# First unit of a fused attention, maxout and rational kernel: the order recomputed, some scaling and weight splitting given to GpSimd

## The chip, the cores and the metric

The kernel runs on one core of one Trainium2 chip. The metric is the device time of one execution in microseconds. The engines are named as the profile names them: PE is TensorE, DVE is VectorE, ACT is ScalarE, POOL is GpSimd, and SP is the engine whose queue issues most loads.

## What is computed

A banded attention (4 batches, 8 heads, 576 positions, 64 per head), whose output `x` goes through a maxout layer and then through a layer with a rational activation. All arithmetic is float32; inputs that the reference keeps as float64 arrive as 64-bit words.

```python
scores = scale * np.matmul(q, k.transpose(0, 1, 3, 2))
mask_plain = (rel >= 0) & (rel < window)                                      # heads 0..3
mask_dil = (rel >= 0) & (rel < window * dilation) & (rel % dilation == 0)     # heads 4..7
attn = np.exp(scores - max); attn = attn / (attn.sum(-1) + 1e-09); attn_out = attn @ v
x = attn_out.transpose(0, 2, 1, 3).reshape(B * S, H * D)                      # 2304 x 512
x = np.maximum(np.maximum(x @ w1, x @ w2), x @ w3) @ w_out                    # 768 wide
h = x @ w_in; P = a0 + a1*h + a2*h*h + a3*h*h*h; Q = 1 + |b0|*|h| + |b1|*h*h  # 2048 wide
out = (P / (Q + 1e-06)) @ w_out2
```

## The kernel before

**Units and parts.** The 2304 tokens of the maxout layer go in five units of 384 or 512. The attention goes in twelve parts of 192 positions, and each part in two groups: `p` (plain band, tiles of 128 queries, 6 of 96 columns) and `d` (dilated band, tiles of 96 queries, 8 of up to 80 columns). Unit 0 needs parts 0 and 1; parts 2 and 3, needed by unit 1, are done beside unit 0's matmuls. Units 1 to 4 follow a fixed pattern that the change leaves alone.

**Steps of a part and group**, with the lines of the kernel before: `S` scores on PE (mask L325, products L341), `MX` maximum on DVE (L369), `D` subtraction on DVE (L385), `E` exponentials on ACT (L393, L397), `SM` row sum on DVE (L404), `SB` scaling by the reciprocal of the sum (L408 to L411 on DVE, or L415 on ACT, one instruction for each tile), `X` transposes on PE (L424), `XC` copy out of PSUM (L433 on DVE or L435 on ACT), `V` products with the values on PE (L447, L455), `VH` and `VL` high and low part of the result (L472 on ACT, L476 on DVE). Part 0's scaled tile is `sb`, part 1 uses spare room in the tiles called `keys`.

**Weights.** Each of the 18 first weights and 6 output weights of the maxout layer arrives as 64-bit words (`L`, SP queue, L534). `up` (ACT, L547) and `bits` (two DVE instructions, L555 and L557) make float32 of it, `hi` (ACT, L571) its high part, `lo` (DVE, L579) the low part. Three matmuls on high and low parts (L597, L598, L599) make one product. `P:n` is such a product for weight n of unit 0, `M:n` the running maximum (ACT L617, DVE L619), `HH` and `HL` the split of the hidden values (L625, L629), `Y` and `YS` the output layer.

**What sets the order.** Unit 0 is written out by hand, word by word, in the table `START`: the words are issued in that order, and each engine runs its own instructions in that order. `W:n` puts 4n small matmuls on a constant tile (`warm`, L207) ahead of the next use of a PSUM bank. Loads of the first unit go through the SP queue and land in the order of issue. POOL has two memsets of zero columns in this stretch (L350: a part at the start of a batch has fewer key columns) and otherwise issues transfers later on.

Of the kernel before, what the change touches and what calls it, by code (L numbers as in the profile page):

```python
# [33 lines left out]


START = """
mk mkB T kp0 qp0 qd0 W:8 S0:p kd0 MX0:p kd1 E0:p W:4 S0:d,mm SM0:p MX0:d qd1 D0:d E0:d SB0:p S1:d
X0:p,1 L SM0:d MX1:d X0:p,0,pv up kp1 qp1 S1:p,mm SB0:d XC0:p,1 bits E1:d L up MX1:p D1:p
XC0:p,0 v0 X0:d,1,sc X0:d,0,pv XC0:d,0 XC0:d,1 W:2 V0:p,mm SB1:d V0:d,sc X1:d,1 bits qd2 v1 E1:p
X1:d,0,mm SM1:p hi lo L L qp2 SB1:p S2:d,pv XC1:d,1 X1:p,0 XC1:d,0 VH0:p VH0:d hi XC1:p,0 L  # L40
X1:p,1,mm VL0:p V1:d,mm L MX2:d up XC1:p,1 VL0:d V1:p,mm VH1:d bits VH1:p VL1:d S2:p VL1:p lo up hi
P:0 up MX2:p L P:1 E2:d lo bits P:2 hi M:0 k1 up bits L SB2:d M:1 lo bits P:3 L hi E2:p up M:2 lo L
bits L hi lo M:3 up HH:0 P:4 X2:d,1,mm bits hi qp3 up hi lo L X2:d,0,pv L SB2:p,act bits S3:p P:5 up
L M:4 lo XC2:d,1 L MX3:p P:6 X2:p,1 qd3 XC2:d,0 S3:d,pv L bits M:5 hi X2:p,0,mm up lo bits P:7 HL:0
up hi M:6 HH:1 lo bits MX3:d up hi XC2:p,0 lo hi L up bits lo M:7 E3:p P:8 P:9 hi bits lo M:8 up
P:12 L L hi bits E3:d lo hi SM3:d M:9 up lo HL:1 HH:2 up XC2:p,1 bits M:12 hi v2 bits L up hi
SB3:d,act P:10 lo M:10 up P:13 L bits P:11 M:13 L SM3:p P:14 V2:p,sc hi HL:2 V2:d,sc SB3:p,act M:11
lo X3:p,0 up lo bits L M:14 hi bits up X3:d,0,pv bits HH:4 XC3:p,0 L X3:d,1,mm hi X3:p,1,pv lo v3
HH:3 lo P:16 HL:4 hi XC3:d,1 lo up P:15 HL:3 up P:17 bits XC3:d,0 VH2:d M:15 bits up XC3:p,1 hi
VH2:p M:16 bits lo V3:p hi M:17 V3:d,tp lo VH3:p hi VH3:d lo HH:5 HL:5 Y:2 VL2:d VL3:d Y:0 YS:0 YS:2  # L50
Y:3 VL3:p YS:3 Y:1 VL2:p YS:1
"""

UNITS = {3: """
# [49 lines left out]
def kernel(  # L104
# [16 lines left out]
    nc = tc.nc  # L121
# [167 lines left out]
    def attn_pieces(c):  # L289
# [12 lines left out]
        def SC(g, pool="sc"):  # L302
            plain = g == "p"
            qT = at_raw.pop((c, g))
            U, Q, W = (2 * BP, 2 * QP, WP) if plain else (8, 2 * M, nmk)
            G = U // 2
            pem = on_pe(g)
            scs = []
            for j in range(2):
                t = bank(pool, "sc")  # L310
                ww = WP if plain else WD
                scs.append(t[:, 0:G * ww].rearrange("p (u w) -> p u w", w=ww)[:Q, :, :W])

# [13 lines left out]
            for n in range(U):
                i, blk = divmod(n, BP)
                if plain:
                    k0 = key0(ci, blk)  # L330
                    lq, rk = qT[:, n, :], kTp[:, k0 // 32:(k0 + WP) // 32, i, :]
                else:
                    lq, rk = qT[:, n, :], kTd[:, m0 // 16:(m0 + nmk) // 16, n, :]
                o = scs[n // G][:, n % G, :]
                o = o.rearrange("q (n t) -> q n t", t=32 if plain else 16)
                for h in (slice(0, QP), slice(QP, Q)) if plain else (slice(0, Q),):
                    if plain and c < EARLY:
                        l, r = lq[h], rk[h]
                    else:
                        l, r = lq[:, h], rk  # L340
                    nc.tensor.matmul(o[h], lhsT=l, rhs=r,  # L341
                                     start=not pem, stop=not pem or n % G == G - 1)
            if c == 1:
                ww = WP if plain else WD
                sb = keys0["x1l" if plain else "x1h"][:Q, 2 * S:2 * S + U * ww]
                sb = sb.rearrange("p (u w) -> p u w", w=ww)
            else:
                sb = at.tile([Q, U, WP if plain else WD], F32, tag="s" + g, bufs=SBB, name="sb")
            if W < WD and not plain:
                nc.gpsimd.memset(sb[:, :, W:WD], 0.0)  # L350
# [50 lines left out]
        def SM(g):  # L401
            sv, Q, W, U, sm = grp[g][:5]
            if mode[g] != "A":
                nc.vector.tensor_reduce(out=sm[:, :, 0], in_=sv, axis=AX.X, op=ALU.add)  # L404

        def SB(g, engine="dve"):
            sv, Q, W, U, sm = grp[g][:5]
            nc.vector.tensor_scalar_add(sm, sm, 1.0e-9)  # L408
            nc.vector.reciprocal(sm, sm)
            if engine == "dve":  # L410
                nc.vector.tensor_tensor(out=sv, in0=sv, in1=sm.to_broadcast([Q, U, W]),  # L411
                                        op=ALU.mult)
# [157 lines left out]
        cv[i][3] = slot  # L570
        nc.scalar.activation(out=slot[:, 0:512], in_=cv[i][2], func=AF.Copy)  # L571

    def cv_lo(i):
        kind, f, j = conv_seq[i]
        _, _, t, slot = cv.pop(i)
        if kind == "w2":
            nc.gpsimd.dma_start(out=w2d[f], in_=t)
        else:
            nc.vector.tensor_sub(slot[:, 512:1024], t, slot[:, 0:512].bitcast(F32))  # L579

    cv_at = {"load": 0, "up": 0, "bits": 0, "hi": 0, "lo": 0}
    cv_steps = (("hi", cv_hi, "bits"), ("lo", cv_lo, "bits"), ("up", cv_up, "load"),
# [112 lines left out]
    with ExitStack():  # L695
# [385 lines left out]
```

## Time and profile before

| | us |
|---|---|
| median of 3 runs | 776.62 (776.45 to 776.84) |
| the profiled execution | 776.12 |
| its span, first to last instruction | 774.3 |
| PE busy in the span | 766.6 (99%) |
| DVE, ACT, POOL busy | 585.3, 452.7, 59.3 |
| granted TensorE clock, all slices | 0.9 or more of full speed |

PE is listed as busy nearly throughout, but the ends of matmuls are modelled in this profile, so a wait is best seen in the distance between the starts of two groups. The chain of waits leads over PE for 97% of the span; the remaining 3% lie in the first 25 us, before the first product with a weight.

### The profile page before, as it was taken

Reading aid. Unit: us, or ns where it says so; the run is one execution under the profiler, and the core shown is the slowest. Engines: PE = TensorE matmul, PEld = TensorE weight load, DVE = VectorE, ACT = ScalarE, POOL = GpSimd, SP = SyncE. Lnnn points to the kernel's source line nnn. Section 1 sums busy time; section 2 is a strip of 40 time slices with the busy share of each in tenths; the row PEclk is TensorE's granted clock in tenths of the full one; section 3 lists DMA queues with packets and bytes.
Section 4 is the critical chain, followed back from the end, with each engine's and each line's share of the span. In section 5 each row is a group of like instructions: output and inputs, shape, how many; then the busy total and the mean of one; then the engine's idle time right before and its main releaser. Section 6 shows DMA issues by size and latency. Waiting matters only on the chain.

```text
span 774.3 us, 12063 instructions
## 1 busy us (share of the span) xinstructions
PE 766.6 (99%) x4656; PEld 660.3 (85%) x4656; DVE 585.3 (76%) x996; ACT 452.7 (58%) x842; POOL 59.3 (8%) x114
## 2 busy tenths in 40 slices
PE   8999999999999999999999999999999999999998
PEld 7999999988888888888888888888888888888996
DVE  6999477567635663455499998889888998888983
ACT  5997243433332333343687878677776768676872
POOL 0000222213121101000000001000000001000010
PEclk9999999999999999999999999999999999999999
DMA  9981577657655557532400011000110001000010
GB/s 344 401 347 50 181 226 239 198 157 234 193 176 173 170 177 237 186 109 92 139 0 1 1 55 55 1 1 3 66 42 1 1 28 55 1 0 1 1 55 27
DMA packets 28634, 85.67 MB, mean 111 GB/s; under 512 B 3680, under 2 KB 5728, under 8 KB 28576
## 3 DMA queue, kind: packets, MB, share of 16 engines
q1 hardware_dynamic: 19344, 52.08, 21.4%
q0 software_dynamic: 8800, 32.51, 11.5%
q8 instruction: 36, 0.59, 0.3%
q10 hardware_dynamic: 432, 0.31, 0.1%
q14 instruction: 22, 0.18, 0.1%
HBM read 67.06 MB, written 17.83 MB: 110 GB/s over the span
## 4 chain that ended last, share of the span: by engine, by line
PE 97%; ACT 1%; DVE 1%; DMA 0%; issue 0%; SPq 0%; ACTq 0%
PE mm L597 13%; PE mm L598 13%; PE mm L599 13%; PE h L597 8%; PE h L599 8%; PE h L598 8%; PE acc L909 8%; PE acc L911 8%; PE acc L910 8%; PE sc L341 3%; PE tpp L424 2%; PE pv L455 1%; PE pv L447 1%; DMA qTp<-in_qf_dram 0%; ACT keys L397 0%; DVE mx L369 0%
## 5 line engine op out<-in xcount | busy, mean ns | idle before, releaser
L597 PE MATMUL mm<-x1h,w1s 128*128 128x512 f32 (+1 forms) x360 | 134.5, 374 | 0.0
L599 PE MATMUL mm<-x1h,w1s 128*128 128x512 f32 (+1 forms) x360 | 132.4, 368 | 0.0
L598 PE MATMUL mm<-x1l,w1s 128*128 128x512 f32 (+1 forms) x360 | 132.4, 368 | 0.0
L599 PE MATMUL h<-x2h,w2s 128*128 128x512 f32 (+1 forms) x280 | 103.0, 368 | 0.0
L598 PE MATMUL h<-x2l,w2s 128*128 128x512 f32 (+1 forms) x280 | 103.0, 368 | 0.0
L597 PE MATMUL h<-x2h,w2s 128*128 128x512 f32 (+1 forms) x280 | 103.0, 368 | 0.0
L909 PE MATMUL acc<-w2s,gh 128*128 128x512 f32 x252 | 98.1, 389 | 0.0
L910 PE MATMUL acc<-w2s,gh 128*128 128x512 f32 x252 | 98.1, 389 | 0.0
L911 PE MATMUL acc<-w2s,gl 128*128 128x512 f32 x252 | 96.2, 389 | 0.0
L857 ACT ACTIVATE q<-h 128x512 f32<-128x512 f32 x72 | 43.1, 598 | 85.5 <-PE h L599 84.1
L597 PEld LDWEIGHTS mm<-x1h,w1s 128*128 128x128 f32 x360 | 67.6, 188 | 9.1
L599 PEld LDWEIGHTS mm<-x1h,w1s 128*128 128x128 f32 x360 | 67.6, 188 | 8.6
L864 DVE SCALAR_TENSOR_TENSOR q<-q,cs,ab 128x512 f32<-128x512 f32 x72 | 54.0, 749 | 27.5 <-ACT ab L858 26.6
L598 PEld LDWEIGHTS mm<-x1l,w1s 128*128 128x128 f32 x360 | 67.6, 188 | 8.1
L619 DVE TENSOR_TENSOR m<-mm,m 128x512 f32<-128x512 f32 (+1 forms) x60 | 38.0, 633 | 35.2 <-PE mm L599 30.5
L599 PEld LDWEIGHTS h<-x2h,w2s 128*128 128x128 f32 x280 | 52.8, 189 | 8.8
L597 PEld LDWEIGHTS h<-x2h,w2s 128*128 128x128 f32 x280 | 52.8, 189 | 8.8
L598 PEld LDWEIGHTS h<-x2l,w2s 128*128 128x128 f32 x280 | 52.7, 188 | 8.8
L859 ACT ACTIVATE p<-h,cs 128x512 f32<-128x512 f32 x72 | 56.5, 785 | 0.4 <-DVE gl L894 0.4
L911 PEld LDWEIGHTS acc<-w2s,gl 128*128 128x128 f32 x252 | 47.3, 188 | 9.9
L910 PEld LDWEIGHTS acc<-w2s,gh 128*128 128x128 f32 x252 | 47.3, 188 | 9.7
L909 PEld LDWEIGHTS acc<-w2s,gh 128*128 128x128 f32 x252 | 47.3, 188 | 9.7
(120 smaller groups left out, 1492.3 us busy)
## 6 DMA issues: line engine op xcount, KB each, us to landing
w1r<-in_w_dram SPq DMA_DIRECT2D x18, 512.0 KB, 9.2
raw<-in_w_in_dram SPq DMA_DIRECT2D x16, 512.0 KB, 4.3
w2d<-cvt POOLq DMA_DIRECT2D x32, 256.0 KB, 4.7
raw<-in_w_out_dram SPq DMA_DIRECT2D x16, 512.0 KB, 4.2
w2s<-w2d SPq DMA_DIRECT2D x28, 256.0 KB, 2.9
vd<-in_vd_dram POOLq DMA_DIRECT2D x8, 512.0 KB, 5.6
x2l<-x2d SPq DMA_DIRECT2D x4, 1024.0 KB, 6.0
out_dram<-ob POOLq DMA_DIRECT2D x16, 256.0 KB, 2.7
```

The costliest lines, as they stand in the source:

```text
L341: nc.tensor.matmul(o[h], lhsT=l, rhs=r, start=not pem, stop=not pem or n % G == G - 1)
L424: nc.tensor.transpose(tp[:, i, :], sv[:, G * j + i, :], ident[:Q, :Q])
L597: nc.tensor.matmul(o, lhsT=lh, rhs=rh, start=(i == 0), stop=False)
L598: nc.tensor.matmul(o, lhsT=lh, rhs=rl, start=False, stop=False)
L599: pe_at[0] = nc.tensor.matmul(o, lhsT=ll, rhs=rh, start=False, stop=(i == n - 1))
L619: nc.vector.tensor_tensor(out=m1[u, f], in0=o, in1=m1[u, f], op=ALU.max)
L857: nc.scalar.activation(out=s["q"], in_=s["h"], func=AF.Square)
L859: nc.scalar.activation(out=s["p"], in_=s["h"], func=AF.Identity, scale=cs[:, 3:4], bias=cs[:, 2:3])
L864: nc.vector.scalar_tensor_tensor(out=s["q"], in0=s["q"], scalar=cs[:, 5:6], in1=s["ab"], op0=ALU.mult, op1=ALU.add)
L909: nc.tensor.matmul(o, lhsT=gh, rhs=w[:, 0:512], start=(c == 0), stop=False)
L910: nc.tensor.matmul(o, lhsT=gh, rhs=w[:, 512:1024], start=False, stop=False)
L911: nc.tensor.matmul(o, lhsT=gl, rhs=w[:, 0:512], start=False, stop=(c == F2 - 1))
```

## The change

The table `START` is replaced by another order of the same words. Four things in the code go with it: `SB` can run its large multiplication on POOL, and does so for both groups of parts 0, 2 and 3 (six multiplications; the addition and the reciprocal stay on DVE); `lo` can run on POOL, and does so for weights 0, 1, 3, 4, 5, 6 and 7; part 3's zero columns are written by DVE behind its row sum, no longer by POOL at its scores; and one copy `XC0:p,0` moves from ACT to DVE. Before, `SB` of part 2 `p` and of part 3 `p` and `d` was on ACT, the others on DVE. The words `W` make 52 small matmuls, 56 before. From the end of unit 0 on, nothing is changed.

```diff
 START = """
-mk mkB T kp0 qp0 qd0 W:8 S0:p kd0 MX0:p kd1 E0:p W:4 S0:d,mm SM0:p MX0:d qd1 D0:d E0:d SB0:p S1:d
+mk mkB T qp0 kd0 kp0 qd0 kd1 qd1 W:8 S0:p qp1 kp1 L MX0:p S0:d,mm W:3 S1:d,pv MX0:d D0:d W:1 S1:p,mm
...
-            if W < WD and not plain:
+            if W < WD and not plain and c != 3:
                 nc.gpsimd.memset(sb[:, :, W:WD], 0.0)
...
             if mode[g] != "A":
                 nc.vector.tensor_reduce(out=sm[:, :, 0], in_=sv, axis=AX.X, op=ALU.add)
+                if c == 3 and g == "d":
+                    nc.vector.memset(grp[g][8][:, :, W:WD], 0.0)
...
-            if engine == "dve":
-                nc.vector.tensor_tensor(out=sv, in0=sv, in1=sm.to_broadcast([Q, U, W]),
-                                        op=ALU.mult)
+            if engine != "act":
+                engine = nc.vector if engine == "dve" else nc.gpsimd
+                engine.tensor_tensor(out=sv, in0=sv, in1=sm.to_broadcast([Q, U, W]), op=ALU.mult)
                 return
...
-    def cv_lo(i):
+    def cv_lo(i, engine=nc.vector):
...
-            nc.vector.tensor_sub(slot[:, 512:1024], t, slot[:, 0:512].bitcast(F32))
+            engine.tensor_sub(slot[:, 512:1024], t, slot[:, 0:512].bitcast(F32))
...
-                    cv_step(op)
+                    cv_step(op, *[nc.gpsimd] * (arg == "pool"))
```

POOL, from its first memset of zero columns to its first transfers; `w1s` is a split weight, `cvt` its float32 form, `sm` the reciprocals. Before:

```order
L350 MEMSET sb 96x8x32 x2
L653 DMA x2d<-xs 128x384 x2
L283 DMA vp_1296<-in_vp_dram 128x768
L284 DMA vd_1297<-in_vd_dram 128x1024
L653 DMA x2d<-xs 128x384 x2
```

And in the change:

```order
L350 MEMSET sb 96x8x32
L414 ISA
L414 TENSOR_TENSOR sb<-sb,sm 128x576
L414 TENSOR_TENSOR sb<-sb,sm 96x8x48
L581 TENSOR_TENSOR w1s_0_454<-cvt,w1s_0_454 128x512
L581 TENSOR_TENSOR w1s_1_519<-cvt,w1s_1_519 128x512
L414 TENSOR_TENSOR sb<-sb,sm 96x640
L581 TENSOR_TENSOR w1s_0_617<-cvt,w1s_0_617 128x512
...
L414 TENSOR_TENSOR sb<-sb,sm 128x576
L655 DMA x2d<-xs 128x384 x2
```

Thirteen two-input instructions now stand ahead of POOL's first transfer, with one instruction listed as ISA in front of them (the built program names it a reload of POOL's library).

DVE, from the maxima of part 0 (`sc` is a score tile) to the scaling of part 1. Before:

```order
L369 TENSOR_REDUCE mx<-sc 128x3 x2
L372 TENSOR_SCALAR mx<-mx 128x6
L404 TENSOR_REDUCE sm<-sb 128x6
L369 TENSOR_REDUCE mx<-sc 96x4 x2
L385 TENSOR_TENSOR sb<-sc,mx 96x4x48 x2
L408 TENSOR_SCALAR sm<-sm 128x6
L409 RECIPROCAL sm<-sm 128x6
L411 TENSOR_TENSOR sb<-sb,sm 128x576
L404 TENSOR_REDUCE sm<-sb 96x8
L369 TENSOR_REDUCE mx<-sc 96x4 x2
```

And in the change:

```order
L369 TENSOR_REDUCE mx<-sc 128x3 x2
L372 TENSOR_SCALAR mx<-mx 128x6
L369 TENSOR_REDUCE mx<-sc 96x4 x2
L385 TENSOR_TENSOR sb<-sc,mx 96x4x48 x2
L404 TENSOR_REDUCE sm<-sb 128x6
L410 TENSOR_SCALAR sm<-sm 128x6
L411 RECIPROCAL sm<-sm 128x6
L369 TENSOR_REDUCE mx<-sc 96x4 x2
L372 TENSOR_SCALAR mx<-mx 96x8
L404 TENSOR_REDUCE sm<-sb 96x8
```

The two multiplications of part 0 are gone from DVE, and the maxima and differences of part 0's dilated group stand ahead of the plain group's row sum.

SP, its first loads (`qTp`, `qTd` are queries, `keys` the keys of the first batch). Before:

```order
L246 DMA keys_146<-in_kp_dram 128x384
L262 DMA qTp_149<-in_qf_dram 128x384
L262 DMA qTd_151<-in_qd_dram 128x768
L250 DMA keys_147<-in_kd_dram 128x384
L250 DMA keys_147<-in_kd_dram 128x768
L262 DMA qTd_250<-in_qd_dram 128x768
L534 DMA w1r_0_276<-in_w_dram 128x512
L246 DMA keys_146<-in_kp_dram 128x768
```

And in the change:

```order
L262 DMA qTp_146<-in_qf_dram 128x384
L250 DMA keys_149<-in_kd_dram 128x384
L246 DMA keys_148<-in_kp_dram 128x384
L262 DMA qTd_152<-in_qd_dram 128x768
L250 DMA keys_149<-in_kd_dram 128x768
L262 DMA qTd_155<-in_qd_dram 128x768
L262 DMA qTp_208<-in_qf_dram 128x384
L246 DMA keys_148<-in_kp_dram 128x768
```

The first six loads are the same six in another order; behind them part 1's plain queries and keys now come before the first weight.

## Rows read from the trace of the kernel before

**Rows 1.** The page: span; busy time by engine; the chain by engine.
```profile
span 774.3 us, 12063 instructions
...
PE 766.6 (99%) x4656; PEld 660.3 (85%) x4656; DVE 585.3 (76%) x996; ACT 452.7 (58%) x842; POOL 59.3 (8%) x114
...
PE 97%; ACT 1%; DVE 1%; DMA 0%; issue 0%; SPq 0%; ACTq 0%
```

**Rows 2.** Timeline of PE: start, us, engine, line, tiles, count, idle before and releaser.
```profile
9.28 1.55 PE L341 MATMUL sc<-keys,qTd 128*96 128x80 f32 x16 [0.33 <-DMA qTd<-in_qd_dram]
11.48 0.86 PE L424 MATMUL tpp<-mk,sb 128*96 128x128 f32 x6 [0.65 <-DVE sb L411]
...
14.35 0.83 PE L424 MATMUL tpp<-mk,sb 96*80 96x96 f32 x8 [0.63 <-ACT keys L397]
...
16.46 0.92 PE L447 MATMUL pv<-pt,vp 96*64 96x64 f32 x24 [0.83 <-ACT pt L435]
...
19.24 1.51 PE L341 MATMUL sc<-keys,qTd 128*96 128x80 f32 x16
21.04 0.83 PE L424 MATMUL tpp<-mk,keys 128*96 128x128 f32 x6 [0.28 <-ACT w1s L571]
...
25.12 0.45 PE L597 MATMUL mm<-x1h,w1s 128*128 128x384 f32 x1
```

**Rows 3.** The chain that ended last, in order of time: start, us, what.
```profile
4.98 1.22 PE sc L341 x24
...
6.99 1.51 ACT sb L397 x6
...
42.71 1.32 PE sc L341 x16
```

**Rows 4.** Busy time by stretch: length, PE, PEld, DVE, ACT, POOL, clock, DMA, GB/s.
```profile
9.28:25.12 15.84, 13.44 (x234) 11.92 (x234) 15.39 (x40) 12.24 (x37) 0.00 (x0) 1.00 1.03 404
25.12:50.00 24.88, 24.88 (x178) 24.42 (x177) 24.23 (x54) 22.79 (x70) 0.31 (x1) 1.00 1.03 404
50.00:75.00 25.00, 25.00 (x242) 24.29 (x240) 24.59 (x51) 22.59 (x59) 0.00 (x0) 1.00 0.35 123
```

**Rows 5.** Groups of DVE by form, 9.28 to 75 us: busy, mean ns, idle.
```profile
L557 DVE SCALAR_TENSOR_TENSOR cvt<-w1r,cvt 128x512 int32<-128x512 int32 x18 | 12.5, 693 | 0.6
L579 DVE TENSOR_TENSOR w1s<-cvt,w1s 128x512 fp32r<-128x512 f32 x18 | 12.2, 680 | 0.0
L555 DVE TENSOR_SCALAR cvt<-cvt 128x512 int32<-128x512 int32 x24 | 10.0, 417 | 0.0
L619 DVE TENSOR_TENSOR m<-mm,m 128x384 f32<-128x384 f32 x12 | 6.6, 547 | 0.0
L557 DVE SCALAR_TENSOR_TENSOR cvt<-wo1r,cvt 128x512 int32<-128x512 int32 x6 | 4.2, 692 | 0.2
L579 DVE TENSOR_TENSOR wo1s<-cvt,wo1s 128x512 fp32r<-128x512 f32 x6 | 3.9, 683 | 0.0
...
L411 DVE TENSOR_TENSOR sb<-sb,sm 96x640 f32<-96x640 f32 x1 | 0.8, 821 | 0.1
...
L411 DVE TENSOR_TENSOR sb<-sb,sm 128x576 f32<-128x576 f32 x1 | 0.8, 759 | 0.0
...
L411 DVE TENSOR_TENSOR sb<-sb,sm 96x384 f32<-96x384 f32 x1 | 0.6, 553 | 0.0
```

**Rows 6.** Groups of ACT by form in the same stretch.
```profile
L415 ACT ACTIVATE sb<-sb,sm 128x96 f32<-128x96 f32 x12 | 3.4, 362 | 0.9 <-DVE sm L409 0.9
```

**Rows 7.** Groups of POOL by form, from the start to 75 us.
```profile
L350 POOL MEMSET sb<- 96x256 f32 x2 | 0.6, 308 | 35.8 <-PE tpp L424 35.5 <-POOLq L1064 0.3
...
L1064 POOL MEMSET const-float32-0.0<- 128x1 f32 x1 | 0.1, 104 | 0.2 <-issue 0.2
```

**Rows 8.** Timeline of POOL at 237 us: a transfer that it issues.
```profile
237.35 0.55 POOL L653 DMA_DIRECT2D x2d<-xs  x1 [4.48 <-ACT xs L652]
```

**Rows 9.** Timeline of DVE at the same moment.
```profile
237.63 0.49 DVE L555 TENSOR_SCALAR cvt<-cvt 128x512 int32<-128x512 int32 x1 [0.33 <-ACT cvt L547]
```

More of the change, by code (lines that the diff above doesn't have):

```diff
@@ L36 @@
 START = """
-mk mkB T kp0 qp0 qd0 W:8 S0:p kd0 MX0:p kd1 E0:p W:4 S0:d,mm SM0:p MX0:d qd1 D0:d E0:d SB0:p S1:d
[L38 to L48, printed above, removed]
@@ L49 @@
-HH:3 lo P:16 HL:4 hi XC3:d,1 lo up P:15 HL:3 up P:17 bits XC3:d,0 VH2:d M:15 bits up XC3:p,1 hi
-VH2:p M:16 bits lo V3:p hi M:17 V3:d,tp lo VH3:p hi VH3:d lo HH:5 HL:5 Y:2 VL2:d VL3:d Y:0 YS:0 YS:2
-Y:3 VL3:p YS:3 Y:1 VL2:p YS:1
+mk mkB T qp0 kd0 kp0 qd0 kd1 qd1 W:8 S0:p qp1 kp1 L MX0:p S0:d,mm W:3 S1:d,pv MX0:d D0:d W:1 S1:p,mm
+E0:p E0:d SM0:p SB0:p,pool X0:p,1 qd2 MX1:d SM0:d SB0:d,pool MX1:p X0:p,0,mm D1:p XC0:p,0,dve E1:d
+W:1 X0:d,0,sc v0 E1:p XC0:p,1 L v1 up qp2 X0:d,1,mm S2:d,pv XC0:d,0 SB1:d SM1:p L XC0:d,1 X1:d,0
@@ new lines @@
+V0:p,mm SB1:p V0:d,sc XC1:d,0 L VH0:p X1:p,0,mm X1:p,1 up XC1:p,0 X1:d,1,sc XC1:p,1 XC1:d,1 VH0:d
+bits VL0:p qp3 hi V1:p,mm bits VL0:d lo:pool VH1:p V1:d,tp S2:p VL1:p VH1:d up VL1:d L L hi k1 up
+MX2:d MX2:p E2:d qd3 bits bits lo:pool hi P:0 SB2:d,pool L lo L P:1 up L bits M:0 S3:p,pv up bits hi
+MX3:p lo:pool hi lo:pool L P:2 L E2:p L P:3 up hi M:1 M:2 up S3:d,mm M:3 bits X2:d,1,sc bits X2:d,0
+hi HH:0 lo:pool up P:4 L MX3:d lo:pool SB2:p,pool E3:d up bits hi HL:0 hi lo:pool XC2:d,0 SM3:d M:4
@@ new lines @@
+bits L P:5 P:6 X2:p,1 hi lo up M:5 X2:p,0,sc lo bits up up L L bits hi E3:p hi M:6 P:7 P:9 lo
+XC2:p,0 SB3:d,pool L v2 bits SM3:p XC2:p,1 lo M:7 P:10 hi up up HH:1 lo bits hi L M:9 SB3:p,pool
+P:11 up bits M:10 lo bits hi P:8 M:11 P:12 L up L hi HH:3 XC2:d,1 lo M:8 lo V2:d,sc bits up V2:p,sc
+bits M:12 hi lo X3:p,1,pv VH2:d up up X3:d,0,pv X3:d,1,mm hi X3:p,0 L HL:1 bits lo bits hi XC3:d,1
+up P:15 HH:2 L hi lo bits lo L P:13 up XC3:p,0 bits M:15 XC3:d,0 up HL:2 M:13 VH2:p hi bits hi L hi
+lo v3 P:14 M:14 P:16 lo M:16 up P:17 bits lo M:17 HH:4 XC3:p,1 V3:p,tp hi HH:5 V3:d VH3:p HL:3 VH3:d
@@ L52 @@
+HL:4 HL:5 lo Y:2 VL3:p Y:1 YS:2 Y:3 YS:1 VL2:d VL2:p VL3:d Y:0 YS:3 YS:0
 """
@@ L719, with cv_step @@
         steps = {n: (fn, after) for n, fn, after in cv_steps}
-        def cv_step(name):
+        def cv_step(name, *engine):
             fn, after = steps[name]
@@ L724, in cv_step @@
             assert name != "lo" or cv_at["lo"] < cv_at["hi"]
-            fn(cv_at[name])
+            fn(cv_at[name], *engine)
             cv_at[name] += 1
```

## The prediction, made before the changed kernel ran

> **What bounds the kernel now.** I read the page first: PE works for 99% of the span and the chain of waits runs over PE for 97% of it [rows 1]. So time can only be won where PE waits, and the profiled execution took 776.12 us, of which 774.3 are span and 1.8 lie around it. Next I read PE's timeline for waits. All that are listed lie ahead of 25.12 us, where PE meets the first product with a weight [rows 2]; after that no matmul waits for another engine. What the reader is to see in rows 2 is the distance between starts, since the ends of matmuls are modelled. Last I read the busy time by stretch: from 25 to 75 us DVE works 24.23 of 24.88 and 24.59 of 25.00 us, and ACT 22.8 and 22.6 [rows 4]. PE doesn't wait there, but the engine that feeds it has no room. Moving anything in this stretch is therefore a matter of DVE's instructions, one by one.
>
> **The start of the gain: PE's waits ahead of the first product.** The two orders can be compared from 9.28 us on, where PE takes up the second dilated scores as their queries land [rows 2]. The same six loads stand ahead of that point in both orders, so the transfers set it alike. Between 9.28 and 25.12 us PE does the same work in both: scores of part 1 and 2, transposes and products of parts 0 and 1, and eight small matmuls. Before, it waited four times in between. The sixteen score matmuls take 1.32 us when nothing follows late [rows 3]. Between 9.28 and 11.48 that leaves 2.20 - 1.32 = 0.88 us for DVE's scaling of part 0. Then 0.63 us are listed for part 1's exponentials and 0.83 us for the copy of the transposed tile. Between 19.24 and 21.04 there are 1.80 - 1.32 = 0.48 us for the next transposes [rows 2]. The sum is 2.82 us. In the new order the first transposes come only behind all scores of part 1, the copies behind those of part 2, and so on: each wait has other PE work in its place. **2.8 us is the most that can be won,** since the load sets 9.28 us and PE is full afterwards.
>
> Ahead of 9.28 us something gets worse and costs nothing. Part 0's plain scores now need the third load of the queue, not the second: 128 x 384 words of 4 bytes are 0.197 MB, at 404 GB/s 0.49 us [rows 4], so they begin at 4.98 + 0.49 = 5.47 us [rows 3]. PE still reaches the second dilated scores before their queries, as the 0.33 us idle there show [rows 2]: the new order has 12 small matmuls there where the old has 16.
>
> **What is given back on PE's path.** No row of before shows POOL reading two tiles, so its price is bounded by what POOL does show: a memset of 96x256 takes 0.308 us and one of a single column 0.104 [rows 7], so a column written costs (0.308 - 0.104) / 256 = 0.80 ns. An instruction with two inputs and one output makes one such pass if the three overlap and three if they don't: for 512 columns 0.51 to 1.33 us, for 576 columns 0.56 to 1.49, for 384 columns 0.41 to 1.03, for 640 columns 0.62 to 1.64. DVE takes 0.680, 0.759, 0.553 and 0.821 for these [rows 5]. Two of POOL's scalings and two of its low parts lie on PE's way to the first product:
> - Part 0 plain: its exponentials end at 6.99 + 1.51 = 8.50 us [rows 3], so now at 9.0. Behind the row sum (as long as a scaling, 0.76) and two short DVE instructions, themselves behind the dilated group's differences, POOL starts at an estimated 10.4 and ends by 11.0 to 11.9. PE comes to these transposes at 9.28 + 1.32 + 1.22 = 11.8 us and, with the small matmuls and the mask in between, about 12.3, behind part 1's plain scores [rows 3]. Hidden, with 0.4 us left at the worst end.
> - Part 0 dilated: its scaling starts at an estimated 12.8 us, behind a maximum of part 1 on DVE, and PE wants it at about 13.2, after the transposes of 0.86 [rows 2]. It ends at 13.2 to 13.8, so the wait is 0 to 0.6; I take 0.15.
> - The low parts of weights 0 and 1: 0.51 to 1.33 for 0.68, from -0.2 to +0.65 ahead of the first product; I take 0.15.
>
> Together 0.3 us (bounds -0.2 to 1.3, since chained steps may miss each other).
>
> **Beside PE's path: DVE and ACT.** DVE loses 7 low parts x 0.680, and scalings of 0.759, 0.553 and 0.821: 6.89 us [rows 5]. It gains part 3's zero columns (0.31 by POOL's row, rows 7) and a copy out of PSUM (0.55, as the maximum from PSUM, rows 5): 6.0 us less in all. ACT loses three scalings, of six or eight instructions of 0.36 us each, some 5 to 7 us [rows 6]. The price is nothing as long as POOL is the cover, and POOL was idle there [rows 4]. So PE's demand, 2.5 us earlier than before, finds its weights ready unless POOL slows DVE down. The zero columns on DVE stand behind a row sum; had they stayed on POOL, they would hold up the scalings behind them.
>
> **Do POOL and DVE disturb each other?** One row of before shows it: while POOL issued a transfer at 237.35, a conversion on DVE took 0.49 us, where the mean is 0.417 [rows 5, 8, 9]: 0.07 us more. Nine of POOL's thirteen instructions fall behind 25 us, and DVE's conversions are 12.5 + 12.2 + 10.0 + 4.2 + 3.9 = 42.8 us of its 64.2 in the stretches of rows 4, or 67% [rows 5]. At 0.07 us for each that meets one, that is 9 x 0.07 x 0.67 = 0.4 us. I take this, because it is the only row in which the two meet. The far bound is the first rival.
>
> The sum: -2.8 + 0.3 + 0.4 = -2.1 us. The median of before is 776.62, 0.5 us above the profiled execution, and the change is put against the median: **774.5 us.**
>
> **The rivals.**
> *POOL and DVE exclude each other* (slower). If a POOL instruction with two inputs shuts out DVE's conversions and low parts for its whole length, DVE loses 67% of POOL's time behind 25 us. At the upper bounds that time is 5 x 1.33 + 1.64 + 1.49 + 1.03 + 1.49 = 12.3 us, so 8.2 us lost against 6.0 us of relief: DVE, which had no room, is 2.2 us later than before and PE with it, 776.6 + 2.2 = 778.8 us. At the lower bounds (4.7 us) it loses 3.2, and the gain stands. It decides at 6.0 / 0.67 = 9.0 us, 1.0 us an instruction: above it the kernel is slower. For it speaks that POOL's memset rate makes more than one pass likely, and that the low parts follow the conversions closely. Against it: the one meeting in the rows cost 0.07 us, not the rest of POOL's 0.55.
> The Trainium skill has this very rule (SBUF — State Buffer, Who interferes with whom): a DVE instruction with two SBUF inputs contends with a GpSimd instruction that reads SBUF, and whichever starts first holds the shared port to its end. No run here shows that pair yet. The skill also puts a two-input GpSimd instruction at about 2.6 cycles an element (GPSIMD Engine Reference, Elementwise), an estimate of 1.1 us and more for 512 columns; by both the rival's time would be about 778.
>
> *POOL begins late* (slower). The ISA instruction ahead of POOL's first multiplication isn't in the trace of before. POOL is free from the end of its first memset at 1.1 us, and is needed at 10.4 us, so up to 9.3 us of it is hidden, and 0.4 to 1.3 us more by the room above. Each us beyond goes onto PE's path one for one; above some 12.5 us the kernel is slower, and at 15 us it would be about 779.
> The Trainium skill gives about 6 us for the first call into freshly loaded code on this engine (GPSIMD Engine Reference, Instruction dispatch); by that the load is hidden.
>
> *The waits come back under other names* (no change). The dependencies between 12 and 28 us are close in the new order (the copy that moves to DVE, part 1's scalings, the first low parts). If four of them miss by 0.4 us each, 1.6 of the 2.8 us are gone: 775.5 to 776.5.
>
> **How the numbers follow.** A difference of 0.2% is 1.55 us and about what a measurement of this kernel can tell from none. The forecast, a gain of 1.6 to 2.9 us, has a chance of 0.43. Exclusion has 0.37, of which 0.27 is slower by over 1.55 us and 0.10 lies within, at shorter instructions. The late start has 0.06, slower. Waits that come back have 0.14, within. So faster 0.43, same 0.24, slower 0.33. The forecast's own range is 773.7 to 775.1. The range of 8 in 10 must take in most of exclusion: from 773.4, just past the most that can be won, to 779.6, just past exclusion at its upper bounds; a late start and a longer exclusion lie outside.
>
> **What would show it.** Right: PE's timeline takes up the second dilated scores at about 9.3 us again, has no wait over 0.6 us behind that, and meets the first product at about 22.5 us; POOL's thirteen instructions take 0.5 to 1.5 us each; DVE's conversions keep 0.417 and 0.693 us, and DVE has some 5 us idle up to 75 us. Wrong by exclusion: DVE rows for L557, L559 and L581 (their lines in the change) start late or last over 1 us while POOL works, and PE waits for DVE between 27 and 60 us. Wrong by a late start: POOL's first multiplication starts behind 11 us and PE waits for it. Wrong by returning waits: the first product at 24 us or later.

## The result, and the profile after

The changed kernel takes **780.61 us** in the median of 6 runs (779.6 to 781.41), against 776.54 us before, in the median of the 6 runs beside it; the ratio is 1.0054, with a 95% interval from 1.0041 to 1.0067. It is slower by about 4.1 us, where 774.5 us were forecast, and the range (773.4 to 779.6) does not hold it. The profiled execution took 780.62 us, 778.9 of them span; the span is 4.6 us longer than that of [rows 1].

Helpers' lines moved by two: the conversions are now L557 and L559, the low parts L581, the scalings L414, the maxima of the products L621. First the engines from 25 to 75 us, by stretch, and their sum and mean over the four (after, then before; columns as in [rows 4]).

```profile
25.00:35.00 10.00, 9.30 (x69) 8.25 (x68) 9.79 (x17) 8.75 (x37) 5.29 (x4) 1.00 1.03 400
35.00:45.00 10.00, 7.64 (x48) 7.45 (x48) 9.69 (x20) 6.18 (x18) 5.18 (x4) 0.83 1.03 409
45.00:57.00 12.00, 11.95 (x71) 11.58 (x71) 11.73 (x24) 9.40 (x22) 1.70 (x2) 1.00 0.78 311
57.00:75.00 18.00, 17.96 (x154) 17.43 (x153) 17.73 (x34) 14.50 (x30) 0.28 (x1) 1.00 0.30 96
sum 50.00, PE 46.85 PEld 44.71 DVE 48.94 ACT 38.84 POOL 12.45; mean PE 11.71 PEld 11.18 DVE 12.23 ACT 9.71 POOL 3.11
```
```profile
25.00:35.00 10.00, 10.00 (x63) 9.88 (x59) 9.69 (x21) 9.67 (x39) 0.00 (x0) 1.00 1.03 400
35.00:45.00 10.00, 10.00 (x92) 9.54 (x91) 9.76 (x23) 8.54 (x20) 0.31 (x1) 1.00 1.03 408
45.00:57.00 12.00, 12.00 (x71) 11.95 (x70) 11.76 (x26) 11.59 (x32) 0.00 (x0) 1.00 0.88 346
57.00:75.00 18.00, 18.00 (x202) 17.34 (x200) 17.73 (x36) 15.70 (x40) 0.00 (x0) 1.00 0.19 53
sum 50.00, PE 50.00 PEld 48.72 DVE 48.94 ACT 45.50 POOL 0.31; mean PE 12.50 PEld 12.18 DVE 12.23 ACT 11.37 POOL 0.08
```

DVE's column is the one to read. It is busy for 48.94 of 50 us in both, but in that time it works on 92 instructions, where before it was 103 (counted over the 50 us as one stretch; in the rows above, one that crosses a bound stands twice). POOL works 12 us longer, and DVE is no less busy for it. PE, which had no gap here, loses 3.15 us.

The timelines of DVE and of POOL (after, 29 to 36 us) show where it goes: start, duration, engine, line.

```profile
29.19 0.42 DVE L557 TENSOR_SCALAR cvt<-cvt 128x512 int32<-128x512 int32 x1
29.64 1.63 DVE L559 SCALAR_TENSOR_TENSOR cvt<-w1r,cvt 128x512 int32<-128x512 int32 x1
31.20 1.50 DVE L557 TENSOR_SCALAR cvt<-cvt 128x512 int32<-128x512 int32 x1
32.73 1.66 DVE L559 SCALAR_TENSOR_TENSOR cvt<-w1r,cvt 128x512 int32<-128x512 int32 x1
34.32 0.81 DVE L369 TENSOR_REDUCE mx<-sc 128x3 f32<-128x288 f32 x2
35.16 1.27 DVE L372 TENSOR_SCALAR mx<-mx 128x6 f32<-128x6 f32 x1
```
```profile
28.88 1.84 POOL L414 TENSOR_TENSOR sb<-sb,sm 96x640 f32<-96x640 f32 x1 [3.56 <-DMA qTd<-in_qd_dram]
30.69 3.16 POOL L581 TENSOR_TENSOR w1s<-cvt,w1s 128x512 fp32r<-128x512 f32 x2
35.13 1.27 POOL L581 TENSOR_TENSOR w1s<-cvt,w1s 128x512 fp32r<-128x512 f32 x1 [1.29 <-ACT w1s L573]
```

The conversions took 0.417 and 0.693 us in [rows 5]; the last three here take 1.50 and 1.63 to 1.66, and each ends 0.4 to 0.6 us behind the end of a POOL instruction (30.72, about 32.3, 33.85), as if it began only then. The engines take turns: POOL's pair at 30.69 needs 1.58 us each, where one takes 1.28 when DVE doesn't meet it. Even L372, six numbers a partition, lasts 1.27 us, to just behind POOL's end at 36.40.

What reads PSUM is not held (DVE, then POOL, at 44 us): the maximum L621 lies wholly inside POOL's subtraction and takes 0.48 us, no more than the 0.547 of [rows 5]; the conversion behind it is held to 0.75 us and ends 0.29 us behind POOL.

```profile
44.12 0.48 DVE L621 TENSOR_TENSOR m<-mm,m 128x384 f32<-128x384 f32 x1
44.53 0.75 DVE L557 TENSOR_SCALAR cvt<-cvt 128x512 int32<-128x512 int32 x1
```
```profile
43.70 1.29 POOL L581 TENSOR_TENSOR w1s<-cvt,w1s 128x512 fp32r<-128x512 f32 x1 [1.26 <-ACT w1s L573]
```

PE's longest wait is for DVE (PE's waits by releaser: total, times, longest).

```profile
PE sc L325 <- DVE m L621: 2.9, 2, 2.4
PE sc L341 <- DMA keys<-in_kp_dram: 1.2, 1, 1.2
PE sc L207 <- DVE warm L699: 1.0, 1, 1.0
PE tpp L426 <- POOL sb L414: 0.3, 1, 0.3
PE mm L601 <- POOL w1s L581: 0.2, 1, 0.2
PE sc L341 <- DMA qTd<-in_qd_dram: 0.2, 1, 0.2
```

At 34.5 us the scores of part 3 want a bank of PSUM that the maximum L621 still holds, and that maximum stands in DVE's queue behind the rows above. Then the granted clock falls (after, columns as before):

```profile
34.00:36.00 2.00, 0.51 (x3) 0.29 (x3) 1.97 (x4) 1.98 (x4) 0.87 (x1) 1.00 1.03 412
36.00:38.00 2.00, 0.64 (x6) 0.45 (x5) 1.86 (x5) 0.00 (x0) 0.40 (x1) 1.00 1.03 412
38.00:40.00 2.00, 2.00 (x24) 2.00 (x24) 1.97 (x5) 1.30 (x3) 0.59 (x1) 0.88 1.02 408
40.00:42.00 2.00, 2.00 (x8) 2.00 (x8) 1.90 (x6) 1.39 (x7) 1.60 (x2) 0.50 1.04 414
42.00:44.00 2.00, 2.00 (x11) 2.00 (x10) 2.00 (x4) 2.00 (x6) 0.74 (x2) 0.77 1.01 399
```

PE, having mostly stood still from 34.5 to 37.6 us, works at 0.50, the 1.2 GHz level, from about 39.5 us for some 3.4 us. In the kernel before it stays at 1.00 here.

It is neither this wait nor the clock that sets PE's lateness in the end, but a later product (after: ACT, then PE; last the same product in e1, the experiment below that has nothing on POOL).

```profile
55.74 0.63 ACT L573 ACTIVATE w1s<-cvt 128x512 fp32r<-128x512 f32 x1 [1.11 <-DVE sm L410]
56.28 0.47 ACT L619 ACTIVATE m<-mm 128x384 f32<-128x384 f32 x1
```
```profile
56.80 0.44 PE L599 MATMUL mm<-x1h,w1s 128*128 128x384 f32 x1
```
```profile
56.45 0.45 PE L599 MATMUL mm<-x1h,w1s 128*128 128x384 f32 x1 [0.41 <-ACT m L619]
```

PE starts this product as ACT's maximum L619 ends, and ACT has waited 1.11 us for DVE just before. From here to the row in the next section it is 34.9 us in the changed kernel, in its second profile (e8) and in e1, e2 and e3, whatever PE waited for earlier and whether its clock fell. So PE's lateness is DVE's. What the slow clock took from PE is time that it would have waited for DVE, as it does in e1 at full clock.

### The profile page after: what moved, and what is told of

It is laid out like the page before. It is cut to its first block, busy times and chain, and to the rows that moved or that the text cites. A ratio compares the mean times of both kernels' runs of the same rounds, so it can differ in the third digit from the quotient of the medians.

```text
span 778.9 us, 12061 instructions
## 1 busy us (share of the span) xinstructions
PE 769.1 (99%) x4652; PEld 662.0 (85%) x4652; DVE 588.1 (76%) x988; ACT 447.3 (57%) x821; POOL 75.5 (10%) x126
## 4 chain that ended last, share of the span: by engine, by line
PE 92%; DMA 5%; DVE 1%; SPq 0%; issue 0%; ACT 0%
PE mm L599 12%; PE mm L600 12%; PE mm L601 12%; PE h L601 8%; PE h L600 8%; PE h L599 8%; PE acc L913 8%; PE acc L912 8%; PE acc L911 8%; PE sc L341 3%; PE tpp L426 2%; PE pv L457 1%; DMA w1r<-in_w_dram 1%; PE pv L449 1%; DMA vp<-in_vp_dram 1%; DMA kTp<-in_kp_dram 1%
## 5 line engine op out<-in xcount | busy, mean ns | idle before, releaser
L621 DVE TENSOR_TENSOR m<-mm,m 128x512 f32<-128x512 f32 (+1 forms) x60 | 37.9, 632 | 35.1 <-PE mm L601 30.1
```

The source lines that it names most:

```text
L621: nc.vector.tensor_tensor(out=m1[u, f], in0=o, in1=m1[u, f], op=ALU.max)
```

## A common yardstick

Between some 85 and 380 us the lateness of PE that a kernel of this study carries no longer changes (by over 0.02 us at the first scores of the eight units from 87 to 268 us). So each is read at one PE row, the first scores of the next unit (before 87.19, after 91.72: 4.53 us late):

```profile
87.19 1.21 PE L341 MATMUL sc<-kTp,qTp 128*64 128x96 f32 x24
```
```profile
91.72 1.21 PE L341 MATMUL sc<-kTp,qTp 128*64 128x96 f32 x24
```

"DVE lost" below is the sum, over the DVE instructions up to 80 us that overlap an instruction of POOL (those of 0.15 us and less left out), of their duration less the median of the same line and form in the trace before. Ratios are to runs of the kernel before that stood beside each experiment; "late" and "DVE lost" are those of the profiled execution.

| kernel | time, us | ratio to before, 95% | first scores of the next unit | late, us | DVE lost, us |
|---|---|---|---|---|---|
| before | 776.54 | | 87.19 | | |
| changed | 780.61 | 1.0054 (1.0041 to 1.0067) | 91.72 | +4.53 | 7.89 |
| e1 nothing on POOL | 780.41 | 1.0055 (1.0043 to 1.0068) | 91.36 | +4.17 | 0 |
| e2 only scalings on POOL | 779.87 | 1.0048 (1.0036 to 1.0061) | 91.33 | +4.14 | 3.35 |
| e3 only low parts on POOL | 780.43 | 1.0065 (1.0051 to 1.0078) | 90.57 | +3.38 | 3.48 |
| e4 before, one small POOL addition | 778.89 | 1.0032 (1.0019 to 1.0044) | 87.14 | -0.05 | 0 |
| e5 POOL's instructions cut short | 773.69 | 0.9970 (0.9959 to 0.9981) | 85.63 | -1.56 | 0.41 |
| e6 before, seven low parts on POOL | 777.22 | 1.0011 (1.0002 to 1.0020) | 88.08 | +0.89 | 5.18 |
| e7 new order, engines as before | 783.55 | 1.0094 (1.0077 to 1.0111) | 94.77 | +7.58 | 0 |
| e8 changed, again | 780.36 | one run | 91.47 | +4.28 | 7.83 |
| e9 before, nine POOL additions | 788.50 | one run | 95.51 | +8.32 | 8.19 |
| e10 before, nine POOL copies | 780.70 | one run | 89.33 | +2.14 | 2.28 |
| e11 before, nine POOL memsets | 778.16 | one run | 87.28 | +0.09 | 0.53 |
| e12 PE kept at work at 32 us | 780.20 | 1.0048 (1.0031 to 1.0065) | 91.80 | +4.61 | 7.33 |
| e13 loads in the old order | 780.03 | 1.0049 (1.0034 to 1.0064) | 92.32 | +5.13 | 7.55 |

## The experiments

**Theory 1** was the prediction's first rival: POOL and DVE shut each other out, and DVE has no room for it. **Theory 2:** the new order costs by itself. **Theory 3:** POOL's first two-input instruction, with the library load (ISA) ahead of it, slows the first loads; in the changed kernel the plain keys landed at 6.17 us and held up the first scores.

**e1: the new order with nothing on POOL.**
```diff
-E0:p E0:d SM0:p SB0:p,pool X0:p,1 qd2 MX1:d SM0:d SB0:d,pool
+E0:p E0:d SM0:p SB0:p X0:p,1 qd2 MX1:d SM0:d SB0:d
...
-MX2:d MX2:p E2:d qd3 bits bits lo:pool hi P:0 SB2:d,pool
+MX2:d MX2:p E2:d qd3 bits bits lo hi P:0 SB2:d
```
(all six scalings and all seven low parts alike)

> The changed kernel with its new order kept whole, but the six scalings and seven low parts that it gives to GpSimd written to VectorE instead: the new order alone. Theory 1 (VectorE and GpSimd hold each other up): the 2.9 us that the scores wait at 34 us, the clock's fall after it and the stretched VectorE instructions are gone; VectorE's bits take 0.4 to 0.5 us and its low parts 0.7 us everywhere. What is left of the order's own waits (weight 1's low part stands behind both score maxima) is an estimate of 1 to 2 us, against a first product 2 us earlier than before: 776 to 778 us. Theory 2 (the order, not the engine): VectorE is given 12 us more work, so PE waits for it at the same places, 780 us or more. Theory 3 (GpSimd's first two-input instruction slows the loads): the second dilated part of the queries lands at 9.1 us again, and not at 9.8 us, and the first plain scores start at 5.5 us.

Measured: 780.41 us. No DVE instruction is stretched and the clock of the profiled execution stays at 1.0, as theory 1 said, but the time is theory 2's. What holds PE now is DVE's own work (the second wait is for ACT, which at the later of its two places, at 56 us, had waited for DVE):

```profile
PE mm L601 <- DVE w1s L581: 1.9, 1, 1.9
PE mm L599 <- ACT m L619: 1.8, 2, 1.4
```
DVE is again busy for 48.72 of the 50 us. So the run doesn't acquit the exclusion. It says that thirteen instructions on POOL help PE no more than if DVE had done them itself. What they would take there is worked out from [rows 5]: seven low parts of 0.680, three scalings of 0.759, two of 0.553 and one of 0.821, 8.96 us; on POOL they cost DVE 7.89 us of lengthened instructions.

**e2 and e3: one half on POOL each.** (e2: `lo:pool` back to `lo`; e3: `SB..,pool` back to `SB..`)

> The changed kernel with only the seven low parts back on VectorE; GpSimd keeps the six scalings. Theory 1: each side costs by its overlap; of the nine VectorE instructions that were stretched before 57 us about half stand beside a scaling, so about half of the loss is left: 777.5 to 779.5 us, with VectorE stretched at 29 to 31, 41 to 42 and 51 and 56 us alone, and no stall of over 2 us at 34 us. Theory 2 (the order): 780 us as with everything. Theory 3: the loads are as late as in the changed kernel (9.8 us), since a scaling is GpSimd's first two-input instruction here too.

> The changed kernel with only the six scalings back on VectorE; GpSimd keeps the seven low parts. Theory 1: the low parts at 29 to 45 us are those that hold VectorE where PE waits for it, and VectorE now has the scalings too: 779.5 to 781 us, with the stall at 34 to 37 us and probably the clock's fall still there. Theory 2: 780 us. Theory 3: GpSimd's first two-input instruction is now a low part, but the program still stands ready for it at 1 us, so the loads are as late as in the changed kernel (9.8 us).

Measured: 779.87 and 780.43 us. Each half loses DVE 3.4 or 3.5 us, less than half of the whole, but each costs nearly the whole time, so the proportion expected for e2 was wrong: what isn't lost to POOL is done by DVE itself. For e3 a long wait at 34 us and a fall of the clock were expected; PE waited 0.6 us there and the clock stayed at 1.0, yet the kernel takes 780.43 us. The loads also spoke against theory 3: with the same ISA instruction near the start, the plain keys landed at 5.76 us in e2 and at 5.15 in e3.

**e4: the library load alone.**
```diff
+nc.gpsimd.tensor_tensor(out=g[:, 0:1], in0=g[:, 0:1], in1=g[:, 0:1], op=ALU.add)
```


> The kernel before with one addition: a GpSimd addition of one column (128x1) on a tile that nothing else uses, as GpSimd's first instruction after the constants. Nothing waits for it. Theory 3: GpSimd's first two-input instruction slows the first loads by 0.5 to 0.9 us (second dilated query part landing at 9.7 to 10.0 us and not 9.14), and the time goes up by 0.3 to 0.8 us, as far as the waits that follow don't take it up. Theory 1 and theory 2: no difference in landing times, 776.5 us within 0.3 us.

Measured: 778.89 us, yet 0.05 us *early* at 87 us: theory 3 falls. The last query part landed at 9.37 us, not 9.14, and PE made that up before 18 us. The 1.9 us of span come at 383 us, in a row of ACT (e4, timeline):

```profile
382.85 0.69 ACT L878 ACTIVATE ab<-h,cs 128x512 f32<-128x512 f32 x1 [2.03 <-DMA x2d<-xs]
```
Before, the same instruction started at 380.75 and waited for no store. The order of PE and ACT is the same in both. The scratch tile g came into a pool that is reused there; I take it, without a run for it, that it shifted the tiles behind it so that `ab` now lies where `xs` was. e9 to e11 carry g too, so of these only the yardstick at 87 us is used.

**e5: POOL's instructions cut short.**
```diff
+                if engine is nc.gpsimd:
+                    sv, U = sv[:, 0:1], 1
+                    sm = sm[:, 0:1]
...
-            engine.tensor_sub(slot[:, 512:1024], t, slot[:, 0:512].bitcast(F32))
+            engine.tensor_sub(slot[:, a:1024], t[:, a - 512:512], slot[:, a - 512:512].bitcast(F32))
```
(a is 896 on POOL; the products of these weights read the last 128 columns four times)

> The changed kernel, its order and engines kept, with GpSimd's 13 instructions cut short: a scaling takes one head's columns (1/12, or 1/8 for the dilated parts) and a low part 128 of 512 columns; the products of those seven weights read the 128 columns that were written four times. Left out: most of the scaling, and three quarters of seven low parts. GpSimd's work falls from about 16 us to an estimate of 4 us, and VectorE still has none of it. Theory 1 (what GpSimd works, VectorE loses, so that VectorE, which is 97 % busy from 25 to 75 us, gains nothing): the relief of VectorE becomes real, its bits take 0.4 to 0.5 us, the stall at 34 us and the clock's fall are gone, and the kernel comes to 774 to 777 us. Theory 2 (the order itself): PE waits at the same places, 779 us or more.

Measured: **773.69 us**, 0.3% faster than before. This is the run that decides. The order, the engines and the dependencies are those of the changed kernel; only the time for which POOL reads is shorter (0.26 to 0.9 us an instruction). DVE loses 0.41 us and not 7.89, PE is busy for 49.97 of 50 us, and its list of waits is short (all of it):

```profile
PE sc L207 <- DVE warm L709: 1.0, 1, 1.0
PE sc L341 <- DMA keys<-in_kp_dram: 0.4, 1, 0.4
```
PE is 6.1 us earlier at the yardstick than in the changed kernel. Of these, 0.6 stood there already at the first product, where loads had landed sooner, and at most 0.5 are PE's own waits for POOL's results; the rest goes with DVE's loss. So the order does what the prediction said, if DVE really gets the relief. Theory 2 holds only in this form: the order was laid out for a relieved DVE, and is worse than the old one without it.

**e6: one part alone, in the old order.**
```diff
-SM1:p hi lo L L qp2 SB1:p S2:d,pv
+SM1:p hi lo:pool L L qp2 SB1:p S2:d,pv
```
(the first seven `lo` alike)

> The kernel before, its order kept word for word, with one part of the change: GpSimd makes the first seven low parts (128x512 each). Theory 1: VectorE is rid of seven instructions of about 0.7 us (4.9 us) and loses most of seven times 1.28 us (9 us) to them, the more as it is 97 % busy there; PE, which before waited nowhere between 25 and 75 us, waits for 1 to 4 us: 777.5 to 780.5 us, with bits and low parts stretched to 1.2 to 1.7 us. Theory 2 (the new order is what costs): VectorE is relieved and nothing is late, 776.5 us or a little less.

Measured: 777.22 us, +0.11%: the mechanism of theory 1, and PE 0.9 us late where 1 to 4 were expected. DVE lost 5.18 us for a relief of 7 x 0.680 = 4.8 us: a bad bargain of 0.4 us. PE waits 0.6 us, once, for a low part that DVE makes itself.

**e7: the new order, engines as before.** (e1 with `SB2:p,act`, `SB3:d,act`, `SB3:p,act`)

> The changed kernel's order with engines as before: low parts on VectorE, the last three of the six scalings on ScalarE, the first three on VectorE. The order by itself, with nothing on GpSimd. Theory 1: VectorE has about 2 us less than with everything on it, ScalarE 5 us more in a stretch where it is two thirds busy: 778 to 780 us, with no stretched instruction. Theory 2: 780 us or more, since the order was made for other engines, and the waits stand at low parts and maxima.

Measured: 783.55 us, outside what either theory gave. DVE has time here and doesn't get to use it: it waits 4.2 us for ACT's high parts, which stand behind the scalings, and PE waits for both (DVE's waits 25 to 75 us first, then PE's).

```profile
DVE w1s L581 <- ACT w1s L573: 4.2, 2, 2.8
```
```profile
PE mm L599 <- ACT m L619: 2.7, 2, 1.5
PE mm L601 <- DVE w1s L581: 1.9, 1, 1.9
```
In the changed kernel DVE waits for nothing in this stretch. So with the engines as before (but for the zero columns and the one copy, still on DVE) the new order costs 7.6 us by itself: an order belongs to one split of the work.

**e8: the changed kernel again, for its profile.**

> The changed kernel unchanged, a second profile of it. Theory 1: the same stretched VectorE instructions, and PE's wait of 2 to 3 us for the maximum at 34 us. If the clock's fall to 0.5 for 3.4 us after that wait belongs to the mechanism, it is there again; if not, the span is 1 to 2 us shorter at full clock. Theory 3 (GpSimd's first two-input instruction slows the loads): the first plain keys land at 6.2 us again, and the second dilated queries at 9.8 us; if the landings differ by chance, they come at other times.

Measured: the same stretched rows (7.83 us lost), PE's wait for L621 1.6 us in total, the clock at 0.50 again, from 36 to over 42 us. The plain keys landed at 6.41 us, the last queries at 9.40. The clock's low stretch is about twice as long as in the first profile and the span 0.3 us *shorter*, so it can't be added to the loss: PE's wait for L621 is 1.3 us shorter here, and the slower clock fills that time.

**e9, e10, e11: what kind of POOL instruction does it.** Nine instructions of POOL (128x512) are added to the kernel before, on a tile of their own that nobody waits for, between 40 and 66 us.
```diff
+                nc.gpsimd.tensor_tensor(out=g, in0=g, in1=slot, op=ALU.add)   # e9
+                nc.gpsimd.tensor_copy(g, slot)                                # e10
+                nc.gpsimd.memset(g, 0.0)                                      # e11
```


> The kernel before with nine GpSimd additions of two inputs (128x512) added between 37 and 60 us, on a tile that nobody else reads; each starts when a weight's high part is ready. No engine waits for them and no work is moved. Theory 1 (two-input instructions of GpSimd and VectorE's instructions from SBUF hold each other up): VectorE's bits and low parts beside them take 0.8 to 1.7 us and not 0.42 to 0.69, its reads of PSUM (maxima of the products, transposes) keep their time; VectorE loses 6 to 9 us in all, and since it is 97 to 98 % busy there PE is 2 to 6 us late at 80 us. Without exclusion: no stretched instruction, PE on time.

> The same with nine GpSimd copies of one input (128x512) in place of the additions. Theory 1a (only two-input instructions of GpSimd exclude): a copy takes 0.6 to 1.3 us, VectorE is stretched nowhere, PE on time at 80 us. Theory 1b (every GpSimd read of SBUF excludes VectorE): the same stretching as beside the additions, in proportion to the copies' time.

> The same with nine GpSimd memsets (128x512), each started by a copy of one column. Theory 1a and 1b both: writes alone exclude nobody, so VectorE keeps its times but for 0.1 us at the one-column copies, and PE is on time at 80 us. If VectorE is stretched beside the memsets too, it is GpSimd's use of SBUF as such that excludes.

Measured: additions make PE 8.32 us late (more than I expected), copies 2.14, memsets 0.09. Theory 1b is right and 1a wrong: a POOL instruction that reads one SBUF input excludes DVE too, but is half as long. DVE's loss and PE's lateness agree for additions and copies (8.19 and 8.32, 2.28 and 2.14): DVE has no room. Beside the memsets DVE still lost 0.53 us, where 0.1 were expected, and 0.09 of it reached PE. The rows of e9 show that either side may wait (POOL, then DVE): POOL's addition at 58.60 lasts 2.76 us; three DVE instructions run inside it at their usual length, to 60.20, and the fourth takes 1.67 us and ends 0.54 us behind POOL's end at 61.36.

```profile
58.60 2.76 POOL L739 TENSOR_TENSOR g<-g,w1s 128x512 f32<-128x512 f32 x1 [1.88 <-ACT w1s L571]
```
```profile
58.72 0.68 DVE L579 TENSOR_TENSOR w1s<-cvt,w1s 128x512 fp32r<-128x512 f32 x1
59.31 0.55 DVE L629 TENSOR_TENSOR hhl<-m,hhl 128x384 fp32r<-128x384 f32 x1
59.78 0.42 DVE L555 TENSOR_SCALAR cvt<-cvt 128x512 int32<-128x512 int32 x1
60.23 1.67 DVE L557 SCALAR_TENSOR_TENSOR cvt<-w1r,cvt 128x512 int32<-128x512 int32 x1
```
A memset doesn't hold a DVE instruction with two inputs, but it can hold a `tensor_scalar` (e11, POOL, then DVE):

```profile
43.78 0.53 POOL L744 MEMSET g<- 128x512 f32 x1
45.89 0.53 POOL L744 MEMSET g<- 128x512 f32 x1
```
```profile
43.59 0.68 DVE L579 TENSOR_TENSOR w1s<-cvt,w1s 128x512 fp32r<-128x512 f32 x1
45.90 0.54 DVE L372 TENSOR_SCALAR mx<-mx 96x8 f32<-96x8 f32 x1
57.50 0.67 DVE L555 TENSOR_SCALAR cvt<-cvt 128x512 int32<-128x512 int32 x1
```

The low part at 43.59 lies on a memset and keeps its 0.68 us. The small L372 takes 0.54 us for 0.17 and ends 0.02 us behind the memset of 45.89, and L555 takes 0.67 for 0.42 beside one at 57.36: together 0.62 us, more than the net loss. That "writes alone exclude nobody" is thus wrong for these two.

**e12 and e13: the clock, and the start.**
```diff
-P:2 L E2:p L P:3 up hi M:1
+P:2 L E2:p L W:6 P:3 up hi M:1
```
```diff
-mk mkB T qp0 kd0 kp0 qd0 kd1 qd1
+mk mkB T kp0 qp0 qd0 kd0 kd1 qd1
```


> The changed kernel with one word added to its order: 24 small products of zeros (128x128, about 2 us in all) on TensorE ahead of the fourth weight's products, so that TensorE is at work for most of the 2.4 to 2.8 us in which it otherwise waits at 34 us; the wait itself is for VectorE and ends when it did. If the fall of the granted clock (0.5 for 3.4 us, from 39.5 us) follows from TensorE's standing still there, the clock stays at 1.0 and the kernel is 1 to 2 us shorter: 778.5 to 779.5 us. If the clock falls anyway, or the products that are pushed back by 2 us are waited for, 780.3 us or more.

> The changed kernel with the first six loads in the order of the kernel before (plain keys, plain queries, dilated queries, dilated keys). If the start's missing gain (the first product 1.35 us earlier and not 2.8 us) is the load order's, the first plain scores start at 5.0 us and not 6.3 us and the first product comes 0.5 to 1 us earlier, at 22.8 to 23.3 us; VectorE, full from 25 us on, takes most of it up again: 779.8 to 780.6 us. If the landings are late whatever the order, the first product stays at 23.6 to 23.8 us.

Measured: 780.20 and 780.03 us. e12 doesn't settle what makes the clock fall: PE still waited from 34.5 to 36.1 us, and the clock was at 0.50 from about 37 to 44 us. e1 waits 1.9 us ahead of the product at 28.87 us and keeps a clock of 1.0; e2 and e7 wait as long ahead of the same product and their clocks fall (0.83 in the mean from 25 to 35 us). A wait of this length is thus not enough to tell. What the traces do show is that the clock costs next to nothing in these executions, since PE meets DVE's lateness again at the product at 56.8 us (after) or 56.5 us (e8, low for twice as long). The other runs leave a little open: of the six of the changed kernel, three with a mean granted clock of 0.998 took 779.6 to 780.62 us and three with 0.995 or 0.996 took 780.6 to 781.41 us. Only one of the six has a trace, so up to 0.8 us, the distance of the two means, may hang on the clock or on what made it fall. e12's first product came at 22.88 us, 0.9 us ahead of the changed kernel's 23.77, since the plain keys landed at 4.97 us and not at 6.17. At the yardstick it is 0.08 us *later*. e13 began the plain scores at 5.01 us and the first product at 23.52; it is no faster either. None of what is won there arrives. The landings differ between kernels that begin alike; the changed kernel's two profiles have 6.17 and 6.41 us, and what decides isn't shown.

## Why the prediction was wrong

**What bounds the kernel: right, and not taken to its end.** That PE waits nowhere behind 25 us and that DVE has no room was read correctly [rows 4]. But the forecast's 2.8 us are won ahead of 25 us, and DVE has to make up for them in the next 50. The prediction saw that and let it hang on 6.0 us of relief.

**The start: right in its mechanism.** PE needed 13.45 us from the second dilated scores to the first product (10.32 to 23.77, after), 13.2 were forecast and 15.84 measured before [rows 2]: 2.4 of the 2.8 us came. PE took these scores up 1.04 us later than forecast, at 10.32. What failed here, at a smaller price, is "the transfers set it alike": the last load landed between 8.87 and 9.84 us in profiles of the new order, and behind a late third load PE itself was late. e5's first product stands at 23.14 us, two microseconds ahead of before.

**POOL's prices and the path at the start: right.** 1.14 us for 576 columns, 0.82 for 384 and 1.28 for 512 lie within the bounds; 1.84 for 640, beside DVE's conversions, doesn't. PE's waits above list 0.3 us for a scaling at the start, where 0.3 us in all were taken; the 0.2 for a low part stand at 32.5 us, behind the first product.

**POOL and DVE: here it broke.** The step that failed is the price of POOL and DVE meeting, 0.4 us: DVE lost 7.89 us to POOL's thirteen instructions, 6.8 of them behind 25 us, where the term was counted. It took 0.07 us for each POOL instruction that meets a conversion; the trace shows 7.89 / 13 = 0.61 for each of all. The relief of DVE, on which the 2.8 us at the start hung, was eaten by it. The single row that I took for "the two meet" [rows 8] is a transfer that POOL *issues*, not an instruction that works on tiles. It was no evidence on instructions that read, and before has no row of these. With no row, the honest bound was the whole of POOL's time.

**The rival was right, and its price was short by 1.8 us.** It gave 8.2 us lost behind 25 us (6.8 measured there, 7.89 in all) and 778.8 us. Its sum took DVE's balance alone, 2.2 us, as PE's delay. With 7.89 - 6.0 = 1.9 us of deficit PE was 4.5 us late. The difference goes with the order. Worked out in the same way, from [rows 5] and the losses in the table, the new order is later than its deficit by 1.2 to 2.7 us each time (e1: deficit 2.9, late 4.2; e2: 2.1 and 4.1; e3: 1.7 and 3.4), the old order by 0.5 or less (e6: 0.4 and 0.9; e9: 8.2 and 8.3; e10: 2.3 and 2.1). That the new order asks DVE for its work earlier is my reading of this; no run separates it from what else the order changes. The Trainium skill (SBUF — State Buffer, Who interferes with whom) has the rule that a DVE instruction with two SBUF inputs contends with a GpSimd instruction that reads SBUF and not with one that only writes it, and that a DVE instruction with a single SBUF input stays out of it, except in its two-port modes, for which the page names `tensor_scalar`. The traces agree: L559 (two inputs) takes 1.66 us for 0.69 beside POOL's subtraction, the low part 0.68 unchanged beside a memset, L621 0.48 (one input in SBUF, the other in PSUM), and L557, a `tensor_scalar`, is held to 1.50; L372, also a `tensor_scalar`, is held even beside a memset. The prediction cited the rule and gave it 0.37. The rule should have weighed more than a row of another kind.

**The other rivals.** POOL was not late by its own doing: its first scaling started at 11.70 us, behind the 11 us that were to show a late start, but it was released by DVE, so the reload was hidden. e4 shows no price for it at all: POOL's first addition runs from 1.58 to 1.77 us there. Waits came back under other names only through DVE.

**The clock** is in no step of the prediction. It fell after PE's wait; in the profiled executions PE met DVE's lateness again at 56.8 us all the same, so it isn't a term of the sum there.

## What to carry to other kernels

Before work goes from VectorE to GpSimd, ask whether VectorE is full there and what GpSimd reads: beside a VectorE that converts and subtracts in SBUF, 9 us of work moved gave VectorE 1 us back and the kernel nothing. Nine writes (memsets) made PE 0.09 us late here, and VectorE's PSUM reads kept their time beside GpSimd; and count on a new order paying only with the engine split it was laid out for, which a run with the moved instructions cut short tests cleanly. Judge each stage at a row of its own: e4 looked 2.6 us slower for a reason some 380 us behind the edit.

## What was not expected of the hardware

- An instruction as small as L372 (`tensor_scalar`, 6 or 8 numbers a partition, 0.17 us) takes up to 1.27 us beside GpSimd's subtraction, so short rows are held as long ones are. A GpSimd memset, which reads nothing, holds it too (0.54 us, e11).
- A GpSimd copy with one input excludes VectorE too: 1.10 us for a 0.68 us low part (e10, at 43.48), and a copy can itself wait, 2.09 us for 0.62 (at 54.42).
- The granted clock fell to the 1.2 GHz level at the end of a wait of PE or behind it in both profiles of the changed kernel and in e2, e7, e9, e12 and e13, and not in e1, e3, e6 and e10, whose longest waits from 25 to 75 us were 0.6 to 1.9 us. What decides it stays open.
- The same first loads land up to 1.4 us apart (plain keys as the third load: 4.97 to 6.41 us in the six profiles with the reload, 5.28 and 5.61 in the two without the reload).
